# The tail of an attention and spectral-mixing kernel: ACT copies x w of the second tile of each late pair to PSUM, and a pair's two banks are handled by one instruction each

## The chip, the cores and the metric

The kernel runs on one core of a Trainium2 chip. The core has a matrix engine (TensorE: PE, with its weight loads as PEld), a vector engine (DVE), a scalar engine (ACT), GpSimd (POOL), and SyncE (SP), which here only issues DMAs. SBUF is the working memory, with 128 partitions. PSUM is the small memory that PE writes to; a partition of it has eight banks of 512 fp32 values. The metric is the device time of one execution in microseconds (us); lower is better. The kernel before took 430.04 us in the median of three runs (429.88 to 430.52).

## What is computed

The reference, cut to what matters (the 64-wide causal window of the attention and the softmax's details are left out):

```python
q, k, v: (8, 8, 576, 64)              # batch, heads, sequence, head dimension
a = softmax(q k^T / 8, each row sees itself and the 63 before it) v
x = a as (8, 576, 512)                # heads side by side
X = rfft(x, axis=1)[:, :64]           # 64 modes
Y = X * (w_r + i w_i)                 # per mode a 512x512 complex product
y = irfft(Y, n=576)
u = x + y
out = u + max(u @ w_ch, 0)            # fp32, (8, 576, 512)
```

So out = (x + y) + max(x w + y w, 0), with w = w_ch.

## The kernel before, in words

**Stages.** First comes the attention, which gives `x_sb` and `x4`, and the transform of x to 64 modes as matrix products. Then each mode's two 512 x 512 matrices (128 MB of w_r and w_i in fp32) stream through rings of SBUF tiles, and PE multiplies the modes' rows with them (L223, L235, L254). The last 24 modes are done in steps of half a group, two modes a step: L254, 16 matmuls for w_r and 16 for w_i. The last pieces are three loads (L183 to L186). A ring tile is loaded again, by POOL's queue, once PE has used it up.

**The 36 tiles.** The output has 4608 rows in 36 tiles of 128 rows by 512. `tiles` (L927) lists them: eight from each two batches and one that holds the last 64 rows of both. For each tile i:
- `x_jobs` makes `XW[i]` = x w: four transposes (L678), their eviction by ACT (L653), four matmuls with w (L685), the eviction by DVE (L944).
- What is known of y before the last modes is added early for the batches 0 to 3: `add_late` (L884) adds its part of y w to `XW[i]` (matmul L888, DVE L890), and `early_u` (L894) makes `UE[i]` = x + the known part of y (matmuls L902 and L903, then DVE L909 for odd tiles and ACT L913 for even ones).
- `half_job` and `batch_job` transpose and multiply the rows Y of the modes (`put_rows`, L825: matmuls L685, ACT L827 and DVE L828, which write Zall = Y w).

All these are "jobs". `advance()` takes one at a time, between the steps of the modes; the loop at L1108 counts how many are due (`want`, L1156 to L1164): about one a step at first, and many in the last eight half-steps. All that are left are done ahead of the last two (L1128).

**PSUM.** From L605 on the eight banks are five pools of tiles of one bank: "m" 2 (mode products), "t" 2 (transposes and early sums), "y" and "p" 1 each, "z" 2 (products with w). `bank(h)` takes the pool's next tile. Pools of two alternate between their banks.

**Order and waits.** The schedule is by hand: each engine runs its instructions in the order in which the code makes them. The semaphore waits are put in from the tiles: an instruction that writes a tile waits for those that used that tile before, and one that reads it for those that wrote it.

**The tail** begins at L1168. After the last mode product come the last modes' rows (`turn`, `put_first`, `take`; YL, and ZL by the eight matmuls of L1180 and `cast_halves`). Then the tiles are finished in pairs in the order `seq`. The eight pairs in `UE_OF` ("early": batches 0 to 3) need only the last modes' part; the ten others ("late") need all of y. For pair n with its two banks:
- `tail_xw` (L963): one matmul per bank with an identity puts `XW[i]` there (L966);
- `summed` (L1065): the y w part is added (`late_z`, L986, for early pairs; `rows_z`, L1047 or L1050, for late ones), and ACT takes the maximum with 0 in place, bank by bank (L1074);
- `added` (L1076): the y part is added (`late_u`, L979, or `rows_u`, L1021, L1027, L1033), DVE adds `UE[i]` (L1085) or x (L1039) bank by bank, and SP sends each tile out (L996).

The loop at L1195 makes `tail_xw(n)`, `summed(n)`, `added(n - 1)`. Pairs take the pools "tt", "yp", "zz", "mm" in turn. `seq` is four early pairs, then late and early in turn until the early ones are used up, then the other late ones; the last pair is done by `last` (L1090), apart.

Of the kernel before, what the change touches and what calls it, by code (L numbers as in the profile page):

```python
# [9 lines left out]
FP32 = mybir.dt.float32  # L10
FP32R = mybir.dt.float32r
BF16 = mybir.dt.bfloat16
# [14 lines left out]
def kernel(  # L27
# [29 lines left out]
    def pool(name, bufs=1, **kw):  # L57
        opened.append(tc.alloc_tile_pool(name=name, bufs=bufs, **kw))
        return opened[-1]
# [202 lines left out]
    with tc.manual_schedule():  # L262
# [322 lines left out]
        while step < EARLY:  # L585
# [16 lines left out]
        sprE = XL.rearrange("p s b m -> p (s b m)")[:, 0:512].rearrange("p (r h k) -> p r h k", r=2, h=2)  # L602
        trpool = pool("trpool", bufs=2, reuse_waits="tile")

        banks = {"m": pool("ps_mc", bufs=2, space=PSUM, reuse_waits="tile"),  # L605
                 "t": pool("ps_t", bufs=2, space=PSUM, reuse_waits="tile"),
                 "y": pool("ps_y", space=PSUM, reuse_waits="tile"),
                 "p": pool("ps_p", space=PSUM, reuse_waits="tile"),
                 "z": pool("ps_z", bufs=2, space=PSUM, reuse_waits="tile")}

        def bank(h, shape=(128, DM), dtype=FP32, name=None):
            return banks[h].tile(list(shape), dtype, name=name or "ps" + h, tag="bank")


        def inverse_tables():
            ve = nc.vector
# [56 lines left out]
            return Zall[:, b, :]  # L673

        def transposed(src):
            pt = bank("t", [128, NDCH, 128], BF16, "ptx")
            for c in range(NDCH):
                nc.tensor.transpose(out=pt[:, c, :], in_=src[:, c // 2, 128 * (c % 2):128 * (c % 2) + 128],  # L678
                                    identity=ident_bf)
            return evict(pt)  # L680
# [152 lines left out]
        def batch_job(b):  # L833
            def prepare():
                tr = None if b % 2 else cast_rows(b, NM)
                pt = bank("t", [128, NDCH, 128], BF16, "ptx")
                for c in range(NDCH):
                    nc.tensor.transpose(out=pt[:, c, :], in_=YT[:, b, c, :], identity=ident_bf)
                nc.scalar.copy(out=yrows(b), in_=pt.rearrange("p c e -> p (c e)"))
                return tr  # L840

            def done(tr):
                if tr is not None:
                    put_rows(b, NM, tr)

            jobs.append((prepare, done))
# [47 lines left out]
        def early_u(b, cs):  # L894
            def done(_):
                pus = [bank(("yp" if b < 2 else "tm")[j] if len(cs) == 2 else "t") for j in range(len(cs))]
                for c, pu in zip(cs, pus):
                    i = tile_of(b, c)
                    at = tiles[i][1][0][0]
                    halves = pu.rearrange("p (h e) -> p h e", h=2)  # L900
                    if c % 2 == 0:
                        nc.tensor.matmul(out=halves, lhsT=ident_bf, rhs=tiles[i][0], start=True, stop=False)  # L902
                    nc.tensor.matmul(out=pu, lhsT=trigI[:, at:at + 128], rhs=yrows(b), start=(c % 2 == 1),  # L903
                                     stop=True)
                for c, pu in zip(cs, pus):
                    i = tile_of(b, c)
                    if c % 2:
                        UE[i] = spare[2 * b + c // 2]
                        nc.vector.tensor_tensor(out=UE[i].rearrange("p (h e) -> p h e", h=2),  # L909
                                                in0=pu.rearrange("p (h e) -> p h e", h=2), in1=tiles[i][0], op=ALU.add)  # L910
                    else:
                        UE[i] = x_sb[:, c // 2, b].rearrange("p c e -> p (c e)").bitcast(FP32)
                        nc.scalar.copy(out=UE[i], in_=pu)  # L913

            jobs.append((lambda: None, done))
# [19 lines left out]
        def tile_of(b, c):  # L935
            return 9 * (b // 2) + 4 * (b % 2) + c
# [3 lines left out]
        def x_jobs(pl, lo, hi):  # L940
            for i in range(lo, hi):
                def done(tr, i=i):
# [1 line left out]
                    nc.vector.tensor_copy(out=XW[i], in_=multiply(tr))  # L944
                jobs.append((lambda i=i: transposed(tiles[i][0]), done))

        spare = [t[:, i] for hb in range(2) for t in
                 [XQ[hb].rearrange("p s b m -> p (s b m)").bitcast(FP32).rearrange("p (t e) -> p t e", e=DM)]
                 for i in range(4)]
        UE_OF = {tile_of(b, c) for b in range(NLB) for c in range(4)}  # L950
        AA = [(tile_of(b, c), tile_of(b + 2, c)) for b in range(NLB // 2) for c in range(4)]
        BB = [(8, 17), (26, 35)] + [(i, i + 1) for k in range(NLB // 2, B // 2) for i in range(9 * k, 9 * k + 8, 2)]
        assert sorted(i for p in AA + BB for i in p) == list(range(NT))
        X4 = [BB.pop(0) for _ in range(2)]
        seq = [AA.pop(0) for _ in range(4)]
        while AA:
            seq += [BB.pop(0), AA.pop(0)]
        seq += X4 + BB
        ps, pu = {}, {}
        plan = [i for n, p in enumerate(seq) for i in (p if n else p[::-1])]  # L960
        done = {}

        def tail_xw(n, js=(0, 1)):  # L963
            for i in [seq[n][j] for j in js]:
                ps[i] = bank(("tt", "yp", "zz", "mm")[n % 4][seq[n].index(i)])
                nc.tensor.matmul(out=ps[i], lhsT=ident_r, rhs=XW[i], start=True, stop=True)  # L966

        def banks_u(n, of):
            for j, i in enumerate(seq[n]):
                pu[i] = bank(of[j])  # L970

        def alone(i):
            return pu[i] is not ps.get(i)

        def late_u(n):
            for i in seq[n]:
                (at, b), = tiles[i][1]
                r = slice(group_y(b), group_y(b) + 32)
                nc.tensor.matmul(out=pu[i], lhsT=trigL[r, b % 2, at:at + 128], rhs=YL[r], start=alone(i), stop=True,  # L979
                                 skip_group_check=True, tile_position=(group_y(b), 0))  # L980
# [84 lines left out]
        def summed(n):  # L1065
            for i in seq[n]:
                pu[i] = ps[i]
            if seq[n][0] in UE_OF:
                late_z(n)
            else:  # L1070
                for i in seq[n]:
                    rows_z(i)
            for i in seq[n]:
                nc.scalar.activation(out=ps[i], in_=ps[i], func=ACT_F.Relu)  # L1074

        def added(n):  # L1076
            ut = new_ut()
            early = seq[n][0] in UE_OF
            if early:
                late_u(n)  # L1080
            else:
                rows_u(seq[n])
            for j, i in enumerate(seq[n]):
                if early:
                    nc.vector.tensor_tensor(out=ut[:, j], in0=ps[i], in1=UE[i], op=ALU.add)  # L1085
                else:
                    take_rows(i, ut[:, j])
                send(i, ut[:, j])

        def last(n, ut):  # L1090
            for j, i in enumerate(seq[n]):
# [89 lines left out]
                                 rhs=wch[:, c, HALF * h:HALF * h + HALF], start=(c == 0), stop=(c == NDCH - 1))  # L1181
        for g in (2, 3):
            nc.gpsimd.dma_start(out=Yall[rows, 2 * g:2 * g + 2], in_=YL[group_y(2 * g):group_y(2 * g) + 32])
        banks_u(0, "mm")
        late_u(0)
        tail_xw(1)
        cast_halves(ZL, zl)
        late_z(0)
        for g in (2, 3):
            nc.sync.dma_start(out=Zall.bitcast(FP32)[rows, 2 * g:2 * g + 2],  # L1190
                              in_=ZL.bitcast(FP32)[32 * g:32 * g + 32])
        take_z(0)
        summed(1)
        end = len(seq) - 1
        for n in range(2, end):  # L1195
            tail_xw(n)
            summed(n)
            added(n - 1)
        banks_u(end, ("tt", "yp", "zz", "mm")[(end + 1) % 4])
        ut = new_ut()  # L1200
        ut = [ut[:, j] for j in range(2)]
        for j, i in enumerate(seq[end]):
# [37 lines left out]
```

## Time and profile before

| | |
|---|---|
| runs shown, median (lowest to highest) | 430.04 us (429.88 to 430.52) |
| the profiled execution, time | 430.23 us |
| its span, first to last instruction | 428.4 us |
| busy share of the span: PE, DVE, ACT, POOL | 79%, 57%, 43%, 21% |
| last weight piece lands | 393.75 us |
| last mode product ends (L254) | 394.23 us |
| first output DMA issued (L996) | 399.05 us |
| last output DMA issued | 424.65 us |
| output, 36 tiles | 9.44 MB |

The span is shorter than the execution's time by 1.8 us, which lie around it. In the profile, a group's row has line, engine, operation, out<-in by the program's names, shapes and count, then busy us and mean ns of one, then the idle time of the engine just before, with what ended it. A timeline row has start, length, engine, line, operation and the like. Lines (L966) are those of the kernel before unless the text says otherwise. Matmuls are pipelined: the rows of two in a row overlap, and the spacing of their ends is what one costs.

### The profile page before, as it was taken

The page shows a single profiled execution, that of the slowest core. Times are in us where ns is not written, and L with a number is a line of the kernel's source. Part 1 is how long each engine was busy: PE and PEld are TensorE (multiplying, and loading weights), DVE is VectorE, ACT ScalarE, POOL GpSimd, SP SyncE. Part 2 cuts the span into 40 slices and gives each one's busy share as a digit, 9 for nine tenths or more (in the row PEclk, how much of TensorE's full clock was granted, in tenths as well). Part 3 has the DMA queues.
Part 4 walks back from the last instruction along what each step waited for, and adds up shares of the span by engine and source line. Part 5 has one row for each costly group of instructions (what it writes and reads, how often), then busy time and mean ns, then how long its engine had stood idle before and what let it go on. Part 6 is the DMA issues. An engine that isn't in the chain of part 4 may idle for free.

```text
span 428.4 us, 11528 instructions
## 1 busy us (share of the span) xinstructions
PE 336.4 (79%) x5000; PEld 226.7 (53%) x5043; DVE 245.7 (57%) x525; ACT 185.7 (43%) x337; POOL 90.6 (21%) x156
## 2 busy tenths in 40 slices
PE   6898999898999988976627567668676767878994
PEld 5676767676667766662315334345454545445442
DVE  8498887778677765785402212133322334885886
ACT  6575757575676657533301101124222213323772
POOL 8222213122122132112222222211111111120200
PEclk8699999999999999996656888689998998999998
DMA  8999999999999999999999999999999999996797
GB/s 202 212 212 211 211 212 211 212 211 211 211 212 211 212 212 212 211 213 214 213 251 222 213 214 214 206 215 215 214 214 215 215 214 214 214 211 117 264 356 283
DMA packets 37187, 93.29 MB, mean 218 GB/s; under 512 B 2992, under 2 KB 3248, under 8 KB 37136
## 3 DMA queue, kind: packets, MB, share of 16 engines
q0 software_dynamic: 31424, 81.80, 97.8%
q1 hardware_dynamic: 5568, 10.62, 6.8%
q8 instruction: 39, 0.64, 0.5%
q10 hardware_dynamic: 144, 0.13, 0.1%
q14 instruction: 12, 0.10, 0.1%
HBM read 163.58 MB, written 9.44 MB: 404 GB/s over the span
## 4 chain that ended last, share of the span: by engine, by line
DMA 49%; PE 37%; issue 4%; DVE 4%; ACT 4%; POOL 1%; DVEq 0%; ACTq 0%; POOLq 0%
DMA wr<-in_moe_w_r_dram 26%; DMA wi<-in_moe_w_i_dram 23%; PE tr L298 5%; PE s L345 4%; PE s L357 4%; PE pt L365 3%; PE vb L310 3%; PE o L385 2%; PE s L337 2%; PE psz L685 2%; PE psm L254 1%; DVE xw L890 1%; PE psm L223 1%; DMA vd<-in_k_dram 1%; PE px L408 1%
## 5 line engine op out<-in xcount | busy, mean ns | idle before, releaser
L685 PE MATMUL psz<-wch,tr 128*128 128x512 f32 x176 | 57.8, 457 | 10.8 <-DMA wch<-in_moe_w_ch_dram 10.1
L944 DVE CAST xw<-psz 128x512 fp32r<-128x512 f32 x36 | 24.9, 692 | 68.6 <-PE psz L685 68.1
L349 DVE TENSOR_REDUCE mx<-s 128x4 fp32r<-128x512 f32 x72 | 49.4, 687 | 24.7 <-PE s L345 24.4
L653 ACT CAST tr<-ptx 128x512 fp32r<-128x512 bf16 x36 | 21.2, 590 | 80.4 <-PE ptx L678 80.4
L359 ACT ACTIVATE p<-s 128x512 bf16<-128x512 f32 x72 | 39.7, 603 | 12.4 <-PE s L357 12.4
L685 PEld LDWEIGHTS psz<-wch,tr 128*128 128x128 f32 x176 | 34.2, 215 | 17.4 <-issue 10.3
L345 PE MATMUL s<-kT,qT 64*64 64x128 bf16 (+1 forms) x576 | 29.5, 223 | 6.9 <-issue 6.9
L302 ACT COPY kT<-tr 128x576 bf16<-128x576 bf16 x32 | 23.2, 724 | 23.8 <-PE tr L298 23.8
L235 PEld LDWEIGHTS <-XQ 128*64 128x64 bf16 x128 | 14.1, 203 | 30.7 <-issue 25.1
L345 PEld LDWEIGHTS <-qT 64*64 64x64 bf16 x576 | 18.3, 108 | 18.1 <-issue 17.6
L302 ACT COPY qT<-tr 128x576 bf16<-128x576 bf16 x32 | 23.3, 728 | 10.0 <-PE tr L298 10.0
L368 DVE COPY pts<-pt 128x1024 bf16<-128x1024 bf16 (+1 forms) x40 | 25.2, 629 | 3.9 <-PE pt L365 2.3
L357 PE MATMUL s<-mx,ident_r 128*128 128x512 f32 x72 | 26.9, 445 | 0.1
L254 PEld LDWEIGHTS <-XQ 128*32 128x32 bf16 x256 | 9.2, 150 | 29.8 <-issue 29.7
L302 ACT COPY vT<-tr 128x576 bf16<-128x576 bf16 x32 | 23.3, 727 | 3.4 <-PE tr L298 3.3
L749 DVE TENSOR_TENSOR stg<-psm,Yfour 128x512 bf16<-128x512 f32 x10 | 6.9, 691 | 30.4 <-PE psm L235 27.3
L235 PE MATMUL psm<-wi,XQ 128*64 128x512 bf16 x64 | 13.6, 494 | 12.2 <-DMA wi<-in_moe_w_i_dram 12.2
L365 PE MATMUL pt<-ident_bf,p 128*128 128x128 bf16 x288 | 23.0, 221 | 0.2 <-DVE pts L368 0.2
L397 DVE TENSOR_TENSOR x_sb<-o,r 128x512 bf16<-128x512 f32 x32 | 22.1, 692 | 1.1
L285 POOL DMA_DIRECT2D rawk<-in_k_dram x15 | 8.1, 538 | 65.1 <-PE tr L298 59.5
L235 PE MATMUL psm<-wr,XQ 128*64 128x512 bf16 x64 | 14.1, 504 | 8.6 <-DMA wr<-in_moe_w_r_dram 7.1
L184 POOL DMA_DIRECT2D wi<-in_moe_w_i_dram x14 | 9.6, 690 | 50.6 <-PE psm L254 29.3
(294 smaller groups left out, 680.4 us busy)
## 6 DMA issues: line engine op xcount, KB each, us to landing
wi<-in_moe_w_i_dram POOLq DMA_DIRECT2D x21, 1024.0 KB, 14.6
wr<-in_moe_w_r_dram POOLq DMA_DIRECT2D x18, 1024.0 KB, 14.1
wi<-in_moe_w_i_dram POOLq DMA_DIRECT2D x17, 512.0 KB, 19.4
wr<-in_moe_w_r_dram POOLq DMA_DIRECT2D x16, 512.0 KB, 19.4
out_dram<-ut SPq DMA_DIRECT2D x29, 256.0 KB, 2.3
rawv<-in_v_dram POOLq DMA_DIRECT2D x16, 288.0 KB, 15.6
rawk<-in_k_dram POOLq DMA_DIRECT2D x15, 288.0 KB, 14.5
rawq<-in_q_dram POOLq DMA_DIRECT2D x15, 288.0 KB, 14.8
```

Source lines behind the costliest of these rows:

```text
L235: nc.tensor.matmul(out=psm[64 * i:64 * i + 64, :], lhsT=XE.rearrange("k s b m -> k (s b) m")[:, (7 * j + 1 - ri) * B:(7 * j + 9 - ri) * B, ...
L298: nc.tensor.transpose(out=pt[ro, j, :], in_=raw[ro, TH * half + j, :], identity=ident_bf[ro, ro])
L302: nc.scalar.copy(out=to, in_=pt.rearrange("p j n -> p n j"))
L345: nc.tensor.matmul(out=s[ro, t, lo:128], lhsT=lq, rhs=kT[ro, 64 * n - 64 + lo:64 * n + 64], start=False, stop=True, skip_group_check=True)
L349: nc.vector.tensor_reduce(out=mx, in_=s, axis=AX.X, op=ALU.max, negate=True)
L357: nc.tensor.matmul(out=s, lhsT=ident_r, rhs=mx.unsqueeze(2).to_broadcast([128, 4, 128]), start=False, stop=True, skip_group_check=True)
L359: nc.scalar.activation(out=p[:, 4 * c2:4 * c2 + 4, :], in_=s, func=ACT_F.Exp, scale=EX_SCALE)
L365: nc.tensor.transpose(out=pt[:, t, :], in_=st[u]["p"][:, t, :], identity=ident_bf)
L368: nc.vector.tensor_copy(out=ps[:, 0:nt, :], in_=pt[:, 0:nt, :])
L397: nc.vector.tensor_tensor(out=xo.rearrange("p c (h d) -> p c h d", d=64), in0=ov[:, :, :, 0:64], in1=rb, op=ALU.mult)
L685: nc.tensor.matmul(out=pz, lhsT=tr[:, c, :], rhs=wch[:, c, :], start=(c == 0), stop=(c == NDCH - 1))
L944: nc.vector.tensor_copy(out=XW[i], in_=multiply(tr))
```

## The change

Three things in the tail, and what they need:

1. The PSUM pools become four tiles of two banks each (`two`: "m", "t", "yp", "z"); `bank` gives out halves of them, alternating by a counter.
2. The maximum (L1074) and DVE's sum (L1085, L1039) of a pair are one instruction over both banks, from pair 3 on. The pairs 1 and 2 are summed bank by bank (`added_one`). `kept` lays the UE tiles so that those of a pair can be read by one pattern.
3. For nine late pairs (all but the last), ACT copies `XW` of the second tile to its bank (`seed`), two pairs ahead, and PE's identity matmul for that tile goes. The late pairs stand two after each early one ("aaaabbabbabbabbabb").

```diff
-        banks = {"m": pool("ps_mc", bufs=2, space=PSUM, reuse_waits="tile"),
-                 "t": pool("ps_t", bufs=2, space=PSUM, reuse_waits="tile"),
-                 "y": pool("ps_y", space=PSUM, reuse_waits="tile"),
-                 "p": pool("ps_p", space=PSUM, reuse_waits="tile"),
-                 "z": pool("ps_z", bufs=2, space=PSUM, reuse_waits="tile")}
-        def bank(h, shape=(128, DM), dtype=FP32, name=None):
-            return banks[h].tile(list(shape), dtype, name=name or "ps" + h, tag="bank")
+        two = {h: pool("ps_" + h, space=PSUM, reuse_waits="tile").tile([128, 2, DM], FP32, name="ps" + h)
+               for h in ("m", "t", "yp", "z")}
+        side = dict.fromkeys("mtz", 0)
+        def bank(h, shape=None, dtype=FP32):
+            if h in side:
+                t = two[h][:, side[h]]
+                side[h] = 1 - side[h]
+            else:
+                t = two["yp"][:, "yp".index(h)]
...
-        seq = [AA.pop(0) for _ in range(4)]
-        while AA:
-            seq += [BB.pop(0), AA.pop(0)]
-        seq += X4 + BB
+        BB = BB[0:4] + X4 + BB[4:]
+        seq = [{"a": AA, "b": BB}[k].pop(0) for k in "aaaabbabbabbabbabb"]
...
             for i in [seq[n][j] for j in js]:
-                ps[i] = bank(("tt", "yp", "zz", "mm")[n % 4][seq[n].index(i)])
-                nc.tensor.matmul(out=ps[i], lhsT=ident_r, rhs=XW[i], start=True, stop=True)
+                ps[i] = banks_of(n)[:, seq[n].index(i)]
+                if i not in seeds:
+                    nc.tensor.matmul(out=ps[i], lhsT=ident_r, rhs=XW[i], start=True, stop=True)
+        seeds = {p[1] for p in seq[0:-1] if p[0] not in UE_OF}
+        def seed(n):
+            if seq[n][1] in seeds:
+                nc.scalar.copy(out=banks_of(n)[:, 1], in_=XW[seq[n][1]].bitcast(FP32))
...
-            for i in seq[n]:
-                nc.scalar.activation(out=ps[i], in_=ps[i], func=ACT_F.Relu)
+            t = banks_of(n)
+            for t in [t] if n > 2 else [t[:, j] for j in range(2)]:
+                nc.scalar.activation(out=t, in_=t, func=ACT_F.Relu)
...
+            nc.vector.tensor_tensor(out=halves[0], in0=halves[1], in1=left, op=ALU.add)
             for j, i in enumerate(seq[n]):
-                if early:
-                    nc.vector.tensor_tensor(out=ut[:, j], in0=ps[i], in1=UE[i], op=ALU.add)
-                else:
-                    take_rows(i, ut[:, j])
                 send(i, ut[:, j])
+        def added_one(n, j, ut):
+            late_u(n, (j,))
+            i = seq[n][j]
+            nc.vector.tensor_tensor(out=ut[:, j], in0=ps[i], in1=UE[i], op=ALU.add)
+            send(i, ut[:, j])
...
         late_u(0)
-        tail_xw(1)
+        tail_xw(1, (0,))
         cast_halves(ZL, zl)
         late_z(0)
...
+        tail_xw(1, (1,))
         take_z(0)
         summed(1)
+        tail_xw(2)
+        summed(2)
+        ut = new_ut()
+        for j in range(2):
+            added_one(1, j, ut)
+            tail_xw(3, (j,))
         end = len(seq) - 1
-        for n in range(2, end):
-            tail_xw(n)
+        seed(4)
+        for n in range(3, end):
+            if n > 3:
+                tail_xw(n)
             summed(n)
-            added(n - 1)
+            if n + 2 < end:
+                seed(n + 2)
+            if n == 3:
+                ut = new_ut()
+                for j in range(2):
+                    added_one(2, j, ut)
+            else:
+                added(n - 1)
```

## The prediction

> **What bounds the kernel now.** I read the page's chain first, then the 5 us windows of the last 45 us, then timeline and groups of the two stretches that the change touches. The chain:
>
> ```profile
> DMA 49%; PE 37%; issue 4%; DVE 4%; ACT 4%; POOL 1%; DVEq 0%; ACTq 0%; POOLq 0%
> ```
>
> DMA is the weight stream: the last weight piece lands at 393.75 us and PE waits for it at 393.79. PE is mostly the attention at the start and the tail at the end. The windows (length, busy us and count of PE, PEld, DVE, ACT, POOL; clock; DMA share; GB/s):
>
> ```profile
> 375.00:380.00 5.00, 4.08 (x24) 2.09 (x18) 5.00 (x10) 1.80 (x4) 0.71 (x1) 1.00 1.05 208
> 385.00:390.00 5.00, 4.28 (x39) 2.56 (x38) 3.59 (x7) 3.21 (x6) 0.00 (x0) 1.00 1.05 207
> 390.00:395.00 5.00, 3.88 (x48) 2.22 (x47) 1.62 (x4) 0.21 (x1) 0.00 (x0) 1.00 0.36 68
> 405.00:410.00 5.00, 5.00 (x22) 2.52 (x22) 4.37 (x8) 3.67 (x8) 0.00 (x0) 1.00 1.00 368
> ```
>
> Two stages show. Up to 394 the weights fill the DMA queues (1.05), but PE and DVE are nearly as full: the "jobs" (products, row casts, `add_late`, `early_u`) are packed into the last steps, and PE's waits from 354 to 394.3 name the weights for only 2.9 us, 2.1 of them at 354.6. So from 355 on the stage has 0.8 us of slack. From 400 to 422 PE is 100% busy, and the output leaves at 368 GB/s.
>
> Groups from 355.3 to 394.3 (busy, mean ns):
>
> ```profile
> L890 DVE TENSOR_TENSOR xw<-psz,xw 128x512 fp32r<-128x512 f32 x20 | 13.3, 683 | 1.0 <-PE psz L888 1.0
> L888 PE MATMUL psz<-Zall,trigIr 128*128 128x512 f32 x24 | 11.2, 497 | 4.0 <-DVE xw L890 2.5 <-ACT Zall L827 1.2 <-DVE Zall L828 0.2
> L685 PE MATMUL psz<-wch,tr 128*128 128x512 f32 x28 | 9.4, 474 | 0.5 <-DVE tr L821 0.5
> L828 DVE CAST Zall<-psz 64x512 fp32r<-64x512 f32 x7 | 4.9, 694 | 8.3 <-ACT Zall L827 8.3
> ```
>
> And how these use the two psz banks (start, length):
>
> ```profile
> 387.75 0.69 DVE L890 TENSOR_TENSOR xw<-psz,xw 128x512 fp32r<-128x512 f32 x1
> 387.77 1.18 PE L685 MATMUL psz<-wch,tr 128*128 128x512 f32 x4
> ...
> 388.98 0.58 ACT L827 CAST Zall<-psz 64x512 fp32r<-64x512 f32 x1
> 389.59 0.69 DVE L828 CAST Zall<-psz 64x512 fp32r<-64x512 f32 x1 [1.14 <-ACT Zall L827]
> ...
> 390.34 0.49 PE L888 MATMUL psz<-Zall,trigIr 128*128 128x512 f32 x1 [0.23 <-DVE Zall L828]
> ...
> 390.87 0.69 DVE L890 TENSOR_TENSOR xw<-psz,xw 128x512 fp32r<-128x512 f32 x1 [0.59 <-PE psz L888]
> ```
>
> At 387.75 DVE reads one psz bank while PE fills the other.
>
> **Part 1: two banks become one tile (the part that decides).** Before, a bank is a tile of its own, and a matmul waits for the reader of that bank, two users back. In the changed kernel a tile is two banks. The waits in its built program (L892, L894, L832, L907, L913, L706, L707 and, below, L1020 are the changed kernel's numbers of L888, L890, L828, L903, L909, L702, L703 and L1004):
>
> ```
> PE  L892 psz bank 1              waits DVE L832 (reads psz bank 0)
> DVE L894 xw0 <- psz bank 1       waits PE L892
> PE  L892 psz bank 0              waits DVE L894 xw0 (reads psz bank 1)
> PE  L907 pst bank 1              waits DVE L913 (reads pst bank 0)
> ACT L707 tr <- psz bank 1        waits DVE L706 (reads psz bank 0)
> ```
>
> Each user of a pair waits for the last user of either bank, from the start of the mode stage on. Until about 353 there is about one job per weight step of 4.9 us, so that costs nothing: the weight DMA hides it. In the last eight steps it does not. All psz users become one chain. A product link is L685, ACT, DVE, next matmul: 387.77 to 390.34, 2.57 us. An `add_late` link is L888 to L890's start, 0.53, its 0.69 and 0.05 to the next matmul: 1.27. There are 7 products (28/4) and 20 adds (L890), 4 of them with a second matmul of 0.23: 18.0 + 25.4 + 0.9 = 44.3 us. The first L685 starts at 355.93, so the chain ends no earlier than 400.2; before, the last L890 ends at 391.56. From the last L888's start PE still has two weight steps and a turn, 2.5 us by the rows from 390.34 without the weight wait: 400.2 - 1.3 + 2.5 = 401.4, against 394.23 now. That is **+7.2 us at least**. What else PE does in the stretch (L254 6.2, L902/L903 5.3, L838 2.2, L787/L792 1.5: 15.2 us) is hidden where it stands behind a psz matmul whose reader is at work, and exposed where the in-order PE is stuck ahead of it; pst has waits of the same kind. Bounds 0 to half of it (7.6); I take 3.3, since most pieces stand behind such a matmul. Stage: **+10.5 (7.2 to 14.8)**. Weight loads are no second loss: the last is issued at 381.57 and its queue is busy until 388.85 with the one ahead, so several us of lateness are covered.
>
> The Trainium skill, Perfetto Trace Analysis, section Matmuls, says that independent matmul groups should rotate through different PSUM banks, so that one's evacuation overlaps the next one's matmuls. The rows at 387.75 agree, and the changed kernel still rotates banks; by that rule alone this part would cost nothing and the sum would be 433.2, the first rival below, instead of 443.7. What stands against it are the waits, which go by tile.
>
> **Part 2: start of the tail, 394 to 404.** `take` waits for `put_first` too (+0.24: 395.25 against 395.01); L706 for all eight zl products instead of four (0.45), and L707 for L706 (0.43). The second L966 is moved behind `late_z(0)`, which gives 0.4 back; then L1020 waits for ACT's relu of the other bank (0.60). First output: +0.6. Pairs 1 and 2 go bank by bank (`added_one`): relu both 1.07, sum 0.45, add 0.74, sum 0.45, add 0.73 = 3.44, where before 398.41 to 400.75 is 2.34: +1.1; pair 2 +0.5, pair 3's merged add +0.4, by the same rows. Total **+2.6 (1 to 4)**.
>
> **Part 3: the late pairs.** Rows of one cycle of two pairs:
>
> ```profile
> 405.34 0.74 PE L966 MATMUL psm<-xw,ident_r 128*128 128x512 f32 x2
> 406.54 1.07 ACT L1074 ACTIVATE psm<-psm 128x512 f32<-128x512 f32 x2 [0.57 <-PE psm L986]
> 406.87 1.29 DVE L1039 TENSOR_TENSOR ut<-psz,x_sb 128x512 f32<-128x512 f32 x2
> 408.23 0.51 PE L966 MATMUL psy<-xw,ident_r 128*128 128x512 f32 x1
> ```
>
> L966 recurs on psm at 405.34 and on psy at 408.23: 2.89 us per two pairs, 1.445 each, PE without a gap. Nine pairs lose one L966 of 0.234 (spacing of two in a row): 2.1 us. The floor under it is the output: 0.684 us per tile at 383 GB/s (the fullest microseconds), 1.37 per pair. So a pair saves at most 0.08, some 1.0 us over 13 pairs; I take 0.7. ACT gets nine copies from SBUF to PSUM, not in the trace: from the nearest rows 0.58 (L1041) to 0.72 (L302, 576 wide); I take 0.6. The relu of two banks: ACT rows of 256 and 512 elements take 0.37 and 0.58, 0.82 ns an element, so 1.00 (0.9 to 1.16); the add 1.23 (1.1 to 1.38) from 0.42 and 0.69 on DVE. Over three pairs of the new order that is ACT 3 x 0.91 + 2 x 0.5 = 3.7, DVE 3.5 and output 4.1: the output stays the bound, unless ACT's copies take the high end (then +0.1 a pair). A merged relu holds the first bank's sum back by 0.42; before, L979 starts 0.31 after the second relu, so most of that is covered. Sum **-0.7 (-1.0 to +1.0)**.
>
> In the Trainium skill's Perfetto Trace Analysis, Optimizing Scalar/DVE Operations, larger operations help a saturated engine, while breaking them up may help where an engine is not saturated but holds others up. ACT (3.67 of 5.00) and DVE (4.37) are not full here, so it speaks against the merging; by it part 3's 0.7 would be lost, and the sum would be 444.4.
>
> **Part 4: the end.** The last pair's second sum waits for the add of its first, and its second x w matmul for the first's last DVE step (0.69 + 0.45, partly beside the pair before): **+1.1 (0.5 to 1.5)**.
>
> **Sum.** 10.5 + 2.6 - 0.7 + 1.1 = +13.5. The profiled execution took 430.23 us (span 428.4 and 1.8 around it), 0.2 above the median of 430.04. 430.2 + 13.5 = **443.7 us**.
>
> **Rivals.**
> - *Readers and matmuls still overlap in the stream* (the chain of 44.3 is too long because much of it runs before 355, or the weights hide it): parts 2 to 4 alone, 430.2 + 3.0 = 433.2. For it: DMA at 1.05. Against: 0.8 us of slack, and the waits. 7%.
> - *Faster*: PE is the tail's bound, and the nine matmuls go. Output takes 400.0 to 426.5 now, 26.5 us, against 36 x 0.684 = 24.6 if it never pauses: at most 1.8 saved, 428.4. It decides only if all new waits together cost under 1.8, and one `added_one` pair alone is priced at 1.1. 4%.
> - *The change does not do what it says* (ACT's copies cost what PE saves, waits covered): 430, 2%.
> - *Worse*: PE's other work is exposed by more than half, or late steps starve the ring of weight tiles (three slots, each freed by a step): stage +16 to +20, 449 to 454. For it: steps would be 8 us, and PE is in order. Against: loads run two ahead. 17%.
> - Forecast, 438 to 449: 70%.
>
> The range is 435.5 to 451: it leaves out the lower three partly or wholly and the far end of the worse one. A run of this kernel can tell 0.2% (0.9 us) from no change: faster 4%, same 2%, slower 94%.
>
> **What would show it.** Right: PE's L892 waiting mostly for DVE L894 and L832; the two stretches of DVE and PE less busy from 360 on, the weight DMA pausing near the end; the last L254 near 405 with no weight wait; first output near 410; late pairs about 1.37 to 1.45 us apart with output DMA the full engine; ACT's copy about 0.6. Wrong: PE still waiting for the last weights near 394; then part 1 falls, and with it most of the sum.

## The result, and the profile after

The changed kernel takes **457.94 us** in the median of four runs (456.38 to 459.46), the kernel before 430.2 beside it: the ratio is 1.0644 (95% interval 1.0598 to 1.0691). The forecast was 443.7, its range ended at 451. The sign was right; the forecast of +13.5 us was about half of the +27.7 measured. The profiled execution took 456.74 us (span 454.9). Ratios here leave out runs more than 1.5% above the fastest of their kernel (one of four in e3, two of four in e14).

The chain of waits on the page of the changed kernel, by engine:

```profile
DMA 42%; PE 40%; DVE 7%; ACT 5%; issue 4%; POOL 1%; SPq 0%; DVEq 0%; ACTq 0%; POOLq 0%
```

DVE and ACT have grown from 4% each to 7% and 5%: more of the chain now runs through the readers of PSUM. The 5 us windows (columns as before: PE, PEld, DVE, ACT, POOL busy; clock; DMA share; GB/s):

```profile
380.00:385.00 5.00, 3.10 (x28) 1.66 (x28) 2.88 (x6) 1.56 (x3) 0.71 (x1) 1.00 0.51 78
385.00:390.00 5.00, 3.66 (x9) 1.49 (x8) 2.91 (x5) 0.30 (x1) 0.72 (x1) 0.60 1.00 186
390.00:395.00 5.00, 3.88 (x12) 2.05 (x10) 1.72 (x3) 1.36 (x3) 0.00 (x0) 0.50 0.82 156
405.00:410.00 5.00, 3.79 (x32) 2.04 (x31) 2.14 (x4) 2.17 (x4) 0.00 (x0) 0.85 0.00 0
435.00:440.00 5.00, 4.89 (x25) 2.04 (x24) 3.94 (x4) 4.32 (x7) 0.00 (x0) 1.00 1.02 376
```

The weight DMA pauses (0.51, 0.82): a ring tile is loaded again once PE has used it up, and PE is late. In 405 to 410, where the tail was in full swing before, no byte moves. And a column that the forecast's sum left out, the granted clock, falls to **0.50**: in the trace from 368.9 for 3.4 us, from 386.0 for 20.5 us, from 420.1 for 10.2 us, and again at the very end, from 447.4. Only from 435 on is the output at its full rate. The kernel before has one such stretch in the last steps, from 356.2 for 3.4 us:

```profile
355.00:360.00 5.00, 4.47 (x39) 2.96 (x31) 1.78 (x4) 1.67 (x3) 0.72 (x1) 0.66 1.06 213
```

So its profile held the sign; the rows that the forecast priced from came later, at 1.00. PE's longest waits from 355 to 413.5 (us, times, longest):

```profile
PE psz L892 <- DVE xw L894: 4.2, 7, 1.0
PE psz L892 <- DVE Zall L832: 3.7, 3, 1.4
PE psz L689 <- DVE Zall L832: 2.9, 3, 1.4
PE psz L689 <- DVE xw L894: 1.6, 2, 0.8
```

These four were the forecast's sign of the chain. The groups from 355.3 to 413.5:

```profile
L892 PE MATMUL psz<-Zall,trigIr 128*128 128x512 f32 x24 | 14.5, 632 | 7.9 <-DVE xw L894 4.2 <-DVE Zall L832 3.7
L894 DVE TENSOR_TENSOR xw<-psz,xw 128x512 fp32r<-128x512 f32 x20 | 13.8, 689 | 11.1 <-PE psz L892 11.0
L689 PE MATMUL psz<-wch,tr 128*128 128x512 f32 x28 | 9.2, 455 | 4.4 <-DVE Zall L832 2.9 <-DVE xw L894 1.6
```

DVE's add has its old length (689 ns against 683), but idles 11.1 us for PE where it idled 1.0. The matmul's mean rose from 497 to 632 ns: that is the clock. Link by link on the timeline, at full clock and in the stretch of 0.5:

```profile
365.02 1.19 PE L689 MATMUL psz<-wch,tr 128*128 128x512 f32 x4 [1.01 <-DVE Zall L832]
366.25 0.58 ACT L831 CAST Zall<-psz 64x512 fp32r<-64x512 f32 x1 [1.53 <-PE psz L689]
366.86 0.69 DVE L832 CAST Zall<-psz 64x512 fp32r<-64x512 f32 x1 [1.90 <-ACT Zall L831]
367.61 0.49 PE L892 MATMUL psz<-Zall,trigIr 128*128 128x512 f32 x1 [1.17 <-DVE Zall L832]
...
385.98 0.79 PE L892 MATMUL psz<-Zall,trigIr 128*128 128x512 f32 x1 [0.55 <-DVE xw L894]
386.81 0.69 DVE L894 TENSOR_TENSOR xw<-psz,xw 128x512 fp32r<-128x512 f32 x1 [0.29 <-PE psz L892]
387.56 0.80 PE L892 MATMUL psz<-Zall,trigIr 128*128 128x512 f32 x1 [0.79 <-DVE xw L894]
```

The product link is 2.59 us (forecast 2.57); the add link 1.58 in place of 1.27, its matmul 0.79 in place of 0.49. Nothing of psz overlaps any more.

Where the 27.5 us to the last output issue lie (times of the two profiled executions):

| piece | before | after | more |
|---|---|---|---|
| last mode product ends | 394.23 | 413.34 | 19.1 |
| from there to the first output issue | 4.8 | 5.4 | 0.6 |
| 1st to 12th output issue | 7.7 | 13.9 | 6.2 |
| 12th to 32nd | 14.8 | 13.9 | -0.9 |
| 32nd to last | 3.1 | 5.6 | 2.5 |

### The profile page after: what moved, and what is told of

It reads as the page before. It is cut to its first block, busy times and chain, and to the rows that moved or that the text cites. A ratio compares the mean times of both kernels' runs of the same rounds, so it can differ in the third digit from the quotient of the medians.

```text
span 454.9 us, 11475 instructions
## 1 busy us (share of the span) xinstructions
PE 363.7 (80%) x5034; PEld 232.1 (51%) x5034; DVE 246.2 (54%) x511; ACT 190.1 (42%) x332; POOL 90.7 (20%) x156
## 4 chain that ended last, share of the span: by engine, by line
DMA 42%; PE 40%; DVE 7%; ACT 5%; issue 4%; POOL 1%; SPq 0%; DVEq 0%; ACTq 0%; POOLq 0%
DMA wr<-in_moe_w_r_dram 19%; DMA rawk<-in_k_dram 11%; DMA wi<-in_moe_w_i_dram 10%; PE psz L689 5%; PE tr L298 4%; PE s L345 3%; PE pt L365 3%; PE s L357 3%; PE s L337 3%; PE psm L254 2%; PE vb L310 2%; PE psz L892 2%; PE psm L223 2%; PE o L385 2%; DVE xw L894 1%
## 5 line engine op out<-in xcount | busy, mean ns | idle before, releaser
L689 PE MATMUL psz<-wch,tr 128*128 128x512 f32 x176 | 59.7, 466 | 23.3 <-DMA wch<-in_moe_w_ch_dram 11.0
L657 ACT CAST tr<-pst 128x512 fp32r<-128x512 bf16 x36 | 21.2, 588 | 74.2 <-PE pst L682 74.2
L689 PEld LDWEIGHTS psz<-wch,tr 128*128 128x128 f32 x176 | 34.3, 217 | 33.4 <-DMA wch<-in_moe_w_ch_dram 11.2
L337 PE MATMUL s<-mask_t,ident_bf 128*128 128x512 bf16 x72 | 28.4, 395 | 0.6
L302 ACT COPY qT<-tr 128x576 bf16<-128x576 bf16 x32 | 23.3, 728 | 10.2 <-PE tr L298 10.2
L235 PE MATMUL psm<-wr,XQ 128*64 128x512 bf16 x64 | 13.7, 498 | 9.0 <-DMA wr<-in_moe_w_r_dram 5.7
L892 PE MATMUL psz<-Zall,trigIr 128*128 128x512 f32 x24 | 14.5, 632 | 7.9 <-DVE xw L894 4.2
## 6 DMA issues: line engine op xcount, KB each, us to landing
wi<-in_moe_w_i_dram POOLq DMA_DIRECT2D x21, 1024.0 KB, 13.9
wr<-in_moe_w_r_dram POOLq DMA_DIRECT2D x18, 1024.0 KB, 13.9
```

Of the source, the lines that this page charges most:

```text
L235: nc.tensor.matmul(out=psm[64 * i:64 * i + 64, :], lhsT=XE.rearrange("k s b m -> k (s b) m")[:, (7 * j + 1 - ri) * B:(7 * j + 9 - ri) * B, ...
L302: nc.scalar.copy(out=to, in_=pt.rearrange("p j n -> p n j"))
L337: nc.tensor.matmul(out=s, lhsT=ident_bf, rhs=mask_t[:, mk], start=True, stop=True)
L689: nc.tensor.matmul(out=pz, lhsT=tr[:, c, :], rhs=wch[:, c, :], start=(c == 0), stop=(c == NDCH - 1))
L892: nc.tensor.matmul(out=pz, lhsT=trigIr[:, at:at + 128], rhs=zrows(b), start=(n == 0), stop=(n == len(tiles[i][1]) - 1))
```

## The experiments

**Theory A**: the tile-wide waits of the two-bank tiles make the loss, in the stream and in the tail, and the halved clock that follows on PE's gaps enlarges it. **Theory B**: the tail's edits cost the time (copies, merged instructions, order). Rivals within A came up as runs came in: which pair of banks it is, how much is clock, and whether the new start of the tail is dear by waits or by clock. "Tail" below is from the end of the last mode product to the last output issue (30.4 us before, 38.8 after).

**e1: the tiles alone.** The first of the three things, put into the kernel before.

```diff
-        banks = {"m": pool("ps_mc", bufs=2, space=PSUM, reuse_waits="tile"),
...
+        two = {h: pool("ps_" + h, space=PSUM, reuse_waits="tile").tile([128, 2, DM], FP32, name="ps" + h)
+               for h in ("m", "t", "yp", "z")}
```

> The kernel before with one edit: the PSUM pools become four tiles of two banks; the tail is the old one (identity matmuls for both tiles of every pair, one relu and one sum per bank, the old order). Theory A (the loss is made by the waits of the two-bank tiles, in the weight stream and at the start of the tail, and the halved PE clock that follows on the gaps): most of the 27.7 us comes back here, 447 to 458, last mode product near 413 with a stretch of clock 0.5 after 385. Theory B (the edits of the tail cost the time: ACT's copies, merged instructions, the order): 430 to 433, last mode product near 394.

Measured: 458.61 us, ratio 1.0635 (1.0596 to 1.0674), last mode product 417.2. A loss of the whole size is here without any edit of the tail, so B can't be the main cause (what the new start of the tail adds comes with e9, e16 and e17). The clock was at 0.5 in six stretches between 355 and 430, 51 us in all.

**e2, e8, e12: copies and order without the tiles.** e2 has both, e8 the order alone, e12 the copies alone; one-bank tiles, one relu and one sum a bank. The first two added lines are e8, the others e12.

```diff
+        BB = BB[0:4] + X4 + BB[4:]
+        seq = [{"a": AA, "b": BB}[k].pop(0) for k in "aaaabbabbabbabbabb"]
...
+                if i in seeds:
+                    continue
...
+        seeds = {p[1] for p in seq[0:-1] if p[0] not in UE_OF}
+        def seed(n):
+            i = seq[n][1]
+            if i in seeds:
+                ps[i] = bank(("tt", "yp", "zz", "mm")[n % 4][1])
+                nc.scalar.copy(out=ps[i], in_=XW[i].bitcast(FP32))
...
+            if n + 2 < end:
+                seed(n + 2)
```

> The kernel before, its one-bank tiles kept, with ACT's copy of x w for the second tile of nine late pairs and the new order, each bank still with its own relu and sum. Theory A: nothing of the loss is here; nine identity matmuls of 0.234 us go from a PE that was full, and the output is the floor under it: 428.4 to 430.5. Theory B: the copies fill ACT and the order holds pairs up: 433 or more.

> The kernel before with the order of the changed one alone (two late pairs after each early one), no copies by ACT. With copies and order the time was 429.4 against 430.15. If the nine matmuls that ACT's copies take from PE give the gain: 430.0 to 430.4 here. If the order gives it: 429.2 to 429.6.

> The kernel before with ACT's copies for the second tile of nine late pairs and nothing else: the old order, one-bank tiles, one relu and one sum per bank. With copies and the new order it was 429.41, with the order alone 430.0, before 430.15 to 430.2. If the copies alone give the gain: 429.2 to 429.7. If the copies need the late pairs spread evenly (ACT full in the five late pairs at the end of the old order): 429.8 to 430.6.

Measured: e2 429.41 us, 0.9979 (0.9965 to 0.9993); e8 430.0, 1.0000 (0.9991 to 1.0009); e12 429.43, 0.9977 (0.9968 to 0.9986). The copies bring about 0.75 us (0.2%), the order nothing, and the copies do without it. The window from 400 to 420, of the kernel before, then of e2:

```profile
400.00:420.00 20.00, 20.00 (x89) 9.80 (x90) 17.26 (x28) 14.54 (x28) 0.00 (x0) 1.00 0.98 362
```

```profile
400.00:420.00 20.00, 20.00 (x88) 9.27 (x88) 18.06 (x30) 19.17 (x39) 0.00 (x0) 1.00 1.03 381
```

The output goes from 362 to 381 GB/s, nearly the 383 that part 3 took as its ceiling, and ACT from 14.5 to 19.2 of 20 us. PE is still busy for all 20, so these rows don't say which of the three stops the gain there. e2 and e12 are the versions that beat both kernels.

**e3, e4: the chain of psz alone, without and with work in PE's gaps.** e3 is the kernel before with one bank for z (so each user waits for the last); the eighth bank, "w", is used only where modes are spread and in the tail. e4 adds two matmuls for nothing ahead of each of the 27 users of psz in the last eight half-steps.

```diff
-                 "z": pool("ps_z", bufs=2, space=PSUM, reuse_waits="tile")}
+                 "z": pool("ps_z", space=PSUM, reuse_waits="tile"),
+                 "w": pool("ps_w", space=PSUM, reuse_waits="tile")}
...
+        def keep_warm():
+            if warm:
+                junk = bank("w")
+                for c in range(2):
+                    nc.tensor.matmul(out=junk, lhsT=ident_r, rhs=wch[:, c, :], start=True, stop=True)
```

> The kernel before with the pool for products with w cut from two banks to one (the eighth bank stands apart and is used only where the modes are spread and in the tail), so that the readers and the matmuls of psz make one chain; t, m, y and p keep their own banks. Theory A with the chain alone as the cause (7 links of 2.57, 20 of 1.27, 0.9: 44.3 us from 355.9): last mode product 401 to 405, time 438 to 443. Theory A with the clock as amplifier: a stretch of clock 0.5 shows here too, last mode product 405 to 413, time 443 to 450. If the chain of psz is not what matters, but the waits of the other pairs (t, yp, m): under 434.

> As the one-bank z kernel, with two matmuls more (identity by w, into the bank that stands apart, read by nobody) ahead of each of the 27 users of psz in the last eight half-steps: 54 x 0.234 = 12.6 us of PE work for nothing, in the gaps. If the halved clock is what the gaps bring, and it costs over 3 us there: no stretch of clock 0.5 from 370 to 400 and a faster kernel than the one without them, by 1 to 6 us. If the clock is set otherwise or costs nothing: the same time to 5 us slower, the more the less of the added work lies in gaps.

Measured: e3 446.82 us (442.05 to 449.16), 1.0342 (1.0273 to 1.0412), where the clock as amplifier was expected; e4 442.31 (441.73 to 442.6), 1.0273 (1.0252 to 1.0293). From 355 to about the last mode product (409.2 and 406.4), e3 first:

```profile
355.00:409.00 54.00, 38.75 (x274) 19.91 (x269) 27.95 (x49) 13.86 (x27) 5.22 (x8) 0.84 0.78 145
```

```profile
355.00:406.00 51.00, 44.08 (x324) 25.66 (x320) 27.93 (x49) 13.96 (x27) 5.22 (x8) 1.00 0.80 154
```

PE does some fifty matmuls more and the stage ends 2.8 us earlier: the clock stands at 1.00 in place of 0.84. A PE that waits in each link loses its clock, and in e3 that costs the stage 2.8 us at least, since the added work isn't free. One pair of banks as a chain, at full clock, gives 442.3, close to the forecast for all of it.

**e5, e6: all the waits, without and with that work.** e5 is e3 with t, m and yp as two-bank tiles besides; e6 adds the matmuls for nothing.

```diff
+        two = {h: pool("ps_" + h, space=PSUM, reuse_waits="tile").tile([128, 2, DM], FP32, name="ps" + h)
+               for h in ("m", "t", "yp")}
+        banks = {h: pool("ps_" + h, space=PSUM, reuse_waits="tile") for h in "zw"}
```

> The one-bank z kernel (446.8 us, its stretches of clock 0.5 at about 365 to 375 and 380 to 385), and t, m and the pair of y and p made tiles of two banks besides; the old tail. All the waits of the two-bank kernel (458.6) are there again, so if those waits are the whole cause: 455 to 460. If two banks in one tile cost the time in another way than by waits on the last user, it stays near 447.

> The kernel with all the waits, and again two matmuls for nothing ahead of each of the 27 users of psz in the last eight half-steps. For the one-bank z alone these kept the clock at 1.0 in every window and gave back 4.5 us. If the halved clock is what makes the loss larger than the waits themselves: clock 1.0 from 355 to 405, and 443 to 450, against 455 to 460 without them. If the waits of t, m and yp are dear in themselves: within 3 us of the kernel without the added work.

Measured: e5 451.12 us, 1.0477 (1.0452 to 1.0502), short of the 455 expected; e6 446.8, 1.0395 (1.0365 to 1.0426), its clock 1.0 from 355 to 439, the stage's end at 408.1 against 414.05. The three other pairs cost 5.8 us (e5 over e3, by the ratios) and 4.5 (e6 over e4), 2.0 of it in the tail (32.5 against 30.5 in both cases). That e5 misses e1 by 7.5 us is the subject of e15.

**e7, e9, e10, e11: the changed kernel with z's banks apart.** e7 gives z its two one-bank tiles back and keeps everything else; e9 writes the start of the tail as before; e10 makes the identity matmuls of pairs 1 to 3 three times each; e11 makes every relu and sum per bank (as e7 does for the pairs on z, and e9 for pairs 1 and 2). Of the pieces below the first is e7, the next two are e9, then come e10 and e11; e11's is shown against e7.

```diff
-               for h in ("m", "t", "yp", "z")}
+               for h in ("m", "t", "yp")}
+        zpair = pool("ps_z", bufs=2, space=PSUM, reuse_waits="tile")
...
-        tail_xw(1, (0,))
+        tail_xw(1)
...
-            if n == 3:
-                ut = new_ut()
-                for j in range(2):
-                    added_one(2, j, ut)
-            else:
-                added(n - 1)
+            added(n - 1)
...
+                    for _ in range(3 if n in (1, 2, 3) else 1):
+                        nc.tensor.matmul(out=ps[i], lhsT=ident_r, rhs=XW[i], start=True, stop=True)
...
-            for t in [banks_of(n)] if n > 2 and n % 4 != 2 else [half_of(n, j) for j in range(2)]:
+            for t in [banks_of(n)] if False else [half_of(n, j) for j in range(2)]:
```

> The changed kernel with one edit: the two banks of z are tiles of their own again, in the stream and in the tail (every fourth pair has its relu and sum bank by bank); t, m and yp stay tiles of two banks, and the copies, the merged instructions and the order stay. If the chain of psz is what matters in the stream: the last mode product comes back to 394 to 398 without a stretch of clock 0.5 before it, and the time to 430 to 436, of which 1 to 4 are the bank-by-bank start of the tail. If the other three pairs matter as much: 440 or more.

> The kernel with the two banks of z apart (434.95 us, first output 400.4, last 429.2, a stretch of clock 0.5 at 401.6 to 408.5), and the start of the tail written as before the change: pairs 1 and 2 go through the loop like the others, each sum of the early part by one instruction a bank, and the identity matmuls of pair 1 stand together. If the bank-by-bank start is what costs in this tail (priced at 1.6 for the pairs 1 and 2): 431 to 433.5, and the stretch of clock 0.5 goes. If the waits of the two-bank tiles in the loop cost it: 434 to 436.

> As the kernel with the two banks of z apart, with the identity matmuls of the pairs 1, 2 and 3 made three times each, the first two for nothing: 12 x 0.234 = 2.8 us of PE work more, between 396 and 404, most of it ahead of waits for ACT and DVE. If the stretch of clock 0.5 at 401.6 comes from a PE that works too little at the start of the tail and costs there: no such stretch, and 431 to 434 in spite of the work. If it costs nothing or is not to be kept away so: 435 to 438.

> As the kernel with the two banks of z apart, with every pair's relu and sum made by one instruction per bank (t, m and yp stay tiles of two banks). If the merged instructions cost in this tail (a second bank's work held back by 0.4 to 0.5): 432 to 434.5. If they are needed with such tiles, since each instruction waits for the last user of either bank: 436 to 440, late pairs further apart than 1.45.

Measured: e7 434.95 us, 1.0100 (1.0080 to 1.0121), last mode product 395.2, no clock of 0.5 in the job-dense steps. Its groups from 355.3 to 395.3:

```profile
L897 DVE TENSOR_TENSOR xw<-psz,xw 128x512 fp32r<-128x512 f32 x20 | 13.5, 685 | 2.2 <-PE psz L895 1.8
L895 PE MATMUL psz<-Zall,trigIr 128*128 128x512 f32 x24 | 11.6, 510 | 1.6 <-ACT Zall L834 1.0 <-DVE xw L897 0.3 <-DVE Zall L835 0.2
```

DVE's 11.1 us of idle time are 2.2, and the stage ends 1.0 us later than in the kernel before, not 19.1: without the chain on psz nearly all of the stream's loss is gone. The other pairs' waits cost the stage much only on top of that chain (4.8 us from e3 to e5). e9: 433.22 us, 1.0065 (1.0044 to 1.0087), without the stretch of 0.5 at 401.6 that e7 has. e10: 435.56, 1.0123 (1.0109 to 1.0137): here too no clock of 0.5, but no gain, so this didn't tell clock from waits. e11: 437.11, 1.0152 (1.0132 to 1.0172): with tiles of two banks the merged instructions are worth 2.2 us. From the 12th to the 32nd output issue it is 14.6 us against 13.7 in e7; that two instructions on one tile queue up behind each other's users is argued from the waits, not shown apart.

**e13, e14, e16, e17: the changed kernel itself.** e13 adds two matmuls for nothing ahead of each user of psz in the last eight half-steps (into the bank of m that the current mode product leaves free), e14 writes the start of the tail as before, e16 does both, e17 is e13 with the tripled identity matmuls of e10. **e15** is e1 with e13's edit.

```diff
+                for c in range(2):
+                    nc.tensor.matmul(out=two["m"][:, side["psm"]], lhsT=ident_r, rhs=wch[:, c, :], start=True, stop=True)
```

> The changed kernel itself (457.9 us) with two matmuls for nothing ahead of each of the 27 users of psz in the last eight half-steps, into the bank of m that the current mode product does not use: 12.6 us of PE work more. If the halved clock makes a third or more of its loss: clock 1.0 from 355 to the last mode product, that at 405 to 409 in place of 413.3, and 445 to 452. If the waits alone make it: 456 or more.

> The changed kernel with the start of the tail written as before the change (pairs 1 and 2 in the loop, their sums bank by bank after both matmuls, the identity matmuls of pair 1 together). With the banks of z apart this gave back 1.7 us (434.95 to 433.22), and the stretch of clock 0.5 behind the start went. If the new start is a large part of the tail's extra 8.4 us here too (38.8 us from the last mode product to the last output issue, against 30.4 before): 450 to 455. If it is only the waits of the two banks of z and the clock left from the stream: 456 to 459.

> The kernel before with the two-bank tiles alone (458.6 us, clock 0.5 in six stretches from 355 to 430), with the same two matmuls for nothing ahead of each user of psz. If its loss is larger than that of the kernel with the same waits in the stream and z of one bank (451.1) because the clock fell more often, also at the start of the tail: 446 to 452, close to the changed kernel with the added work. If the two-bank tiles themselves cost more at the start of the tail: 453 or more.

> The changed kernel with both edits: the old start of the tail, and the two matmuls for nothing ahead of each user of psz in the last eight half-steps. Each alone gave 453.1 (from 448.3 to 458.5) and 454.5. If the halved clock and the new start make up what the waits alone don't: clock 1.0 from 355 to the end of the tail's work, last mode product near 411, tail near 32.5, 446 to 450, and runs that agree within 2 us. If they overlap, so that one of them suffices: 452 to 455.

> The changed kernel with the new start kept, the matmuls for nothing in the stream, and the identity matmuls of the pairs 1, 2 and 3 made three times each besides (2.8 us of PE work). With the stream's alone it was 454.5, its clock 0.5 from 418.5 to 428.7, its tail 38.6 us from the last mode product to the last output issue. If that halved clock is what makes the new start dear: no such stretch, tail 33 to 36, 450 to 453. If the order of the new start costs by its waits: tail 37 or more, 454 to 457, as where the banks of z stood apart (434.95 and 435.56).

Measured (times in us; stage end and tail from the profiled execution):

| kernel | median | ratio (interval) | clock 0.5 between 355 and 440, from | stage end | tail |
|---|---|---|---|---|---|
| after | 457.94 | 1.0644 (1.0598 to 1.0691) | 368.9, 386.0, 420.1 | 413.3 | 38.8 |
| e13 | 454.48 | 1.0566 (1.0525 to 1.0607) | 418.5 | 411.4 | 38.6 |
| e14 | 453.1 (448.34 to 458.52) | 1.0432 (1.0411 to 1.0453) | 355.4, 372.5, 382.7 | 411.2 | 32.4 |
| e15 | 449.53 | 1.0461 (1.0421 to 1.0501) | none | 410.7 | 33.7 |
| e16 | 449.04 | 1.0434 (1.0414 to 1.0454) | 439.4 | 411.1 | 33.3 |
| e17 | 453.45 | 1.0533 (1.0496 to 1.0570) | none | 412.5 | 37.2 |

e13 fell between its two cases: the clock is at 1.0 to the end of the stage, but that ends only 1.9 us earlier and the kernel gains 3.5 us, an eighth of its loss. e14 is in its first case by the median, and just under it by the ratio, so the new start is a large part of the tail's loss (32.4 us against 38.8). e14 and e16 have the same ratio: with the old start, the added work costs about what the full clock brings. e15 gains 9.1 us over e1.

e15 also answers e5: at full clock the two-bank kernel is at 449.5 and its counterpart e6 at 446.8, so of the 7.5 us between e1 and e5 at most 2.7 are waits, and the rest goes with the clock. Even the 2.7 need not be the kernel's own, since the added matmuls themselves wait in e15, where they write a bank of m, and not in e6, where their bank has no other user in these steps (e15 from 355 to 411, e6 to 408):

```profile
L691 PE MATMUL psm<-wch,ident_r 128*128 128x512 f32 x54 | 19.6, 443 | 2.3 <-DVE stg L784 1.3 <-ACT x_sb L926 0.9
L695 PE MATMUL psw<-wch,ident_r 128*128 128x512 f32 x54 | 19.8, 447 | 0.0
```

e13 and e16 have the same 2.3 us of such waits, which is one reason why their stage ends at 411. e16 against e17 settles the start of the tail. Both keep their clock at 1.0 through it, and still, in 420 to 425, e16 first:

```profile
420.00:425.00 5.00, 4.96 (x20) 2.65 (x21) 4.40 (x4) 4.75 (x7) 0.00 (x0) 1.00 0.90 333
```

```profile
420.00:425.00 5.00, 4.18 (x20) 1.84 (x17) 2.77 (x4) 3.40 (x6) 0.00 (x0) 1.00 0.50 187
```

The new start sends out 187 GB/s where the old one sends 333 (e17's first output is 1.7 us later): it is dear without any halved clock. From the first to the twelfth output issue it takes 11.4 us in e17, 8.2 in e16, 13.9 in the changed kernel: 3.3 us are its order (at most, as e17 carries 2.8 us of added work), and 2.4 or more go with the halved clock. The tail of 37.2 is that of the case "costs by its waits"; the time of 453.45 lies just under it.

## Why the prediction was wrong, point by point

**Part 1 (+10.5, range to 14.8; measured +19.1): the mechanism right, the sum a term short.** The chain is as priced: 7 products and 20 adds, one after the other, links of 2.59 and some 1.3 at full clock (384.69 to 385.98 is 1.29). Along the timeline of psz the 19.1 us are the lower bound of 7.2; 1.3 since the first L689 starts at 357.27, not 355.93; 6.1 in gaps in which psz was free and PE at other work or in other waits (forecast 3.3, its end 7.6); and 4.5 by which the psz matmuls at half clock outlast their rows at full clock. The last is the failed step: the forecast priced every link from rows at clock 1.00 and had no term for a PE that the chain itself slows. The 4.5 are a lower bound, as 3.4 us of the gaps lie at half clock too, where PE's other work also took longer.

e4 and e6 show that the clock costs this stage several us: with 12.6 us of added work it ended 2.8 and 6.0 us earlier than in e3 and e5. e6 has every wait of the two-bank stream and ends the stage at 408.1, inside the range of part 1 (up to 409.0), and its 446.8 us lie inside the whole range too. Executions without added work agree: the stage ends at 411.2 with 17.1 us at half clock (e14, whose stream is that of the changed kernel), at 413.3 with 23.9 (the changed kernel), at 417.2 with 38.3 (e1, the same waits). What the stage takes at full clock without added work was not run; an estimate by the rows is 413.3 - 4.5 = 408.8, at the edge of the range, or less.

The rival "worse" fits the stage (+16 to +20), but neither the time (449 to 454 against 457.9) nor the cause: of PE's 15.2 us of other work at most 6.1 were exposed, less than half, and PE waited 1.0 us for weights.

**Part 2 (+2.6; measured 0.6 + 6.2).** The first output came 0.6 late, as summed. The pairs behind it were mis-sized: priced at 2.0, the new order costs up to 3.3 at full clock (e17 against e16); pair 2, priced at 0.5, pays much like pair 1: in e17 DVE's two adds start 1.2 us apart in both. 2.4 more come with the clock of 0.5 from 420.1, and 0.4 from the tiles (8.2 in e16 against 7.7).

**Part 3 (-0.7; measured -0.9, and -0.75 alone in e12).** Right: ACT's copy took 0.585 us, the merged relu 1.01, the merged add 1.23. The Trainium skill's advice to break operations up where an engine isn't saturated (Perfetto Trace Analysis, Optimizing Scalar/DVE Operations) would have taken the 0.7 away; e11 shows the other way, 2.2 us for the merging, on tiles of two banks. Merging on one-bank tiles wasn't tried, as it needs the wide tile.

**Part 4 (+1.1; measured +2.5).** The two waits named there, on the timeline of the changed kernel:

```profile
446.02 0.68 DVE L1055 TENSOR_TENSOR ut<-psz,x_sb 128x512 f32<-128x512 f32 x1
446.76 0.38 PE L1033 MATMUL psz<-x_sb,ident_bf 128*128 128x256 bf16 x2 [1.51 <-DVE ut L1055]
...
449.23 0.68 DVE L1120 SCALAR_TENSOR_TENSOR ut<-psyp,ut 128x512 f32<-128x512 f32 x1
449.97 0.79 PE L973 MATMUL psyp<-xw,ident_r 128*128 128x512 f32 x1 [1.12 <-DVE ut L1120]
```

PE stands 1.51 and 1.12 us; little of it lies beside the pair before, as had been assumed, and from 447.4 the clock is at 0.5 (0.79 for a matmul). At full clock (e15, with the old tail) the piece is still 5.3 us against 3.1 before.

**Rivals.** *The change does not do what it says* and *streams overlap* (433.2) fall with the result and e1, and with the latter the result that the Trainium skill's rule on rotating banks (Perfetto Trace Analysis, Matmuls) would have given: the banks did rotate, the waits went by tile. *Faster* gave the right price (at most 1.8; e12 has 0.75) and the right condition: its gain is there only without the waits.

## What to carry to other kernels

Before joining PSUM banks into one tile, list who else uses them: every user then waits for the last user of either bank, and where PE and a reader alternated over two banks, that is a chain of matmul, reader, matmul over the whole stretch, far from the place that wanted the wide tile. When a change makes PE wait in short pieces, price the matmuls at the halved clock as well, for the rows that a price is taken from may all be at full clock. To test whether a clock is part of a loss, add matmuls that nobody reads in the gaps: if a kernel with more work is faster, it is. The other way round it proves nothing: in e16 the added work cost about what the clock gave back.

## What the runs showed of the hardware

The halved clock needs no long pause. Windows of the changed kernel: one of 3.41 us behind which the clock stays at 1.00, the 3.41 us ahead of its stretch of 0.5 at 368.9, those ahead of the stretch at 386.0, and that stretch itself:

```profile
355.26:358.67 3.41, 1.96 (x24) 1.20 (x23) 1.45 (x3) 1.06 (x3) 0.71 (x1) 1.00 1.07 216
365.51:368.92 3.41, 1.81 (x7) 0.60 (x5) 2.03 (x4) 0.58 (x1) 0.00 (x0) 1.00 1.05 213
382.57:385.98 3.41, 1.72 (x20) 0.72 (x19) 2.46 (x5) 1.17 (x3) 0.72 (x1) 1.00 0.96 168
385.98:406.46 20.48, 16.61 (x75) 7.59 (x75) 8.81 (x15) 4.32 (x9) 1.63 (x3) 0.50 0.71 125
```

In the second and third PE is busy for half of the 3.41 us, with no wait above 1.4 us in the stage, and loses the clock; in the fourth it is busy for 81% of 20.48 us and stays at half. In the first, with only a little more (57%), it keeps it. In the kernel before the last two of the 3.41 us windows have 2.97 and 2.67 us, and the clock stays at 1.00. All stretches but the last of an execution are whole multiples of 3.41 us (3.4, 6.8, 10.2, 13.7, 17.1, 20.5). It isn't a threshold of the busy rows alone: e7 dropped at 401.6 after windows of 91% and 92%, in which most matmuls stand alone, and the row of one that stands alone is 0.5 long where its spacing in a series is 0.23.

The Trainium skill, TensorE: Matmul & The Clock Gate, Part 1, gives a free-running window of about 3.4 us and half rate after an idle one; the lengths agree, the idle window doesn't, since these were half busy: by that rule the clock would have stayed at 1.00 and the stage ended near the 408.8 estimated above. The Trainium skill's section on psum-queue depth-cycling, of the same page, tells of short pauses between matmul groups that make the clock swing, and the trace agrees.
